# A spectral convolution and two gated MLPs: the second convolution in 20 units, in written order, and tiles 4 and 5 as a fourth pair

## The chip, the cores and the metric

The kernel runs on one core of one Trainium2 chip. A core has a matrix engine (TensorE, PE below), which multiplies out of SBUF into the eight banks of PSUM; three engines for everything else, VectorE (DVE), ScalarE (ACT) and GpSimd (POOL); and SyncE (SP), which here issues most of the transfers from and to memory. Each engine works off its own list of instructions in order and waits for the others by semaphores. The metric is the device time of one execution in microseconds, lower is better.

## The reference

The input x is 2 x 3008 x 256. A circular convolution over the 3008 positions is followed by two gated MLPs on the 6016 rows:

```python
X = np.fft.rfft(x, axis=1)
y = np.fft.irfft(X * (filt_r + 1j * filt_i)[None], n=3008, axis=1)   # 2 x 3008 x 256
t = y.reshape(6016, 256)
t = (1.0 / (1.0 + np.exp(-(t @ w_gate))) * (t @ w_val)) @ w_out      # d_ff 1536
h = t @ w_in                                                         # d_ff 2048
out = (h * (1.0 / (1.0 + np.exp(-1.702 * h)))) @ w_out2
```

The weights come as 64-bit floats and are decoded on the chip. To keep the precision, an operand is held as two parts, a high part (rounded by ACT) and a low part (the rest, by a subtraction on DVE or POOL), and a product is three matmuls, high by high, high by low and low by high (`mm3`, L123 to L126).

## The kernel before

**Tiles.** The 6016 rows are twelve tiles, six for each of the two sequences; two of each six have 480 columns instead of 512 (tiles 4, 5, 10 and 11). A tile of the first MLP needs, for each of twelve f-blocks of 128, 18 matmuls: the gate product `pg` and the value product `pv` (two row halves, three matmuls each: 12), and the back product with `w_out` (6). Around them a sigmoid on ACT, the gate product on DVE (`sg`, L591), the high part `g` on ACT (L120) and its low part `g` on POOL (L121). The back product of a unit is issued on PE two units later (`push`, `depth`).

**Pairs.** Tiles 6 to 11 are handled two at a time: the 2 x 2 blocks of weights and of the pair's columns are multiplied by seven block products instead of eight. One f-block of a pair then costs 21 matmuls and 12 for the back products, instead of 2 x 18. It needs sums of the pair's columns (`Forms`), each in two parts, and sums of the weight blocks (`combine_w1`, for each f-block one sum of 512 columns, `whole`, four of 128 and their parts). `Forms` and weight sums are done as small pieces ("chores") between the products of the sets before.

**The stage that the change touches.** The first sequence is convolved at the head, so its tiles 0 to 5 are ready. While PE multiplies tiles 2 to 5, the second sequence is convolved: the class `Conv` with steps `a1` (transform of a group's x, by `four`, whose results DVE transposes and splits into the parts `ap`), `c1` (three matmuls; ACT copies the halves swapped into `v`, DVE multiplies by the filter's real part, L536, POOL `v` by its imaginary part, L537, DVE adds both, and `yp` are the two parts of the sum), `d1` (three matmuls, and a transposition `z`) and `e1` (`four` again; two transpositions `tt` and the stores). `c1` and `d1` come 16 times, `a1` and `e1` eight times. The filter's rows are spread by copies on ACT and given their sign on POOL (`sign_f`, L394 to L398).

There are 44 units in the stage: tiles 2 and 3 with ten f-blocks each, tiles 4 and 5 with twelve. One step of the convolution is spread over two units, `a1` and `d1` in one and `c1` and `e1` in the other, so that the 16 steps take 40 units. `c1` writes bank 7, `d1` bank 6, `a1` banks 3 and 6, `e1` banks 7 and 3; `pg` and `pv` take banks 0 to 2 in turn, and the back products 4 and 5. In this stage the framework's scheduler decides the order on each engine; behind it (and in the head) the order is the written one. The weight sums of the first two f-blocks (`sum_ahead`) come in units 35 to 38, the forms of the first pair (tiles 6 and 7) in the units after the convolution. The unit loop is:

## Time and profile before

| | |
|---|---|
| median of 3 runs | 1146.67 us (1145.49 to 1146.74) |
| the profiled execution's own time | 1145.9 us |
| its span, first to last instruction | 1144.1 us |
| PE busy | 1134.6 us, 99% |
| DVE busy | 675.5 us, 59% |
| ACT busy | 646.1 us, 56% |
| POOL busy | 406.5 us, 36% |

The profile is of one execution. The span is what the rows of the trace fill; some 1.8 us lie around it. A matmul's row in the trace is longer than its share of the time, because the next one is started before it ends: what it costs is read from start to start. A DVE or ACT row overlaps its successor by some 0.1 us for the same reason. An engine's busy row can hold waiting: an instruction that has begun and is held up counts as busy.

### The profile page before, as it was taken

The page shows a single profiled execution, that of the slowest core. Times are in us where ns is not written, and L with a number is a line of the kernel's source. Part 1 is how long each engine was busy: PE and PEld are TensorE (multiplying, and loading weights), DVE is VectorE, ACT ScalarE, POOL GpSimd, SP SyncE. Part 2 cuts the span into 40 slices and gives each one's busy share as a digit, 9 for nine tenths or more (in the row PEclk, how much of TensorE's full clock was granted, in tenths as well). Part 3 has the DMA queues.
Part 4 walks back from the last instruction along what each step waited for, and adds up shares of the span by engine and source line. Part 5 has one row for each costly group of instructions (what it writes and reads, how often), then busy time and mean ns, then how long its engine had stood idle before and what let it go on. Part 6 is the DMA issues. An engine that isn't in the chain of part 4 may idle for free.

```text
span 1144.1 us, 14519 instructions
## 1 busy us (share of the span) xinstructions
PE 1134.6 (99%) x5108; PEld 912.7 (80%) x5108; DVE 675.5 (59%) x1154; ACT 646.1 (56%) x1226; POOL 406.5 (36%) x338
## 2 busy tenths in 40 slices
PE   9999999999999999999999999999999999999998
PEld 4378887777788788888888888888888888888887
DVE  6989985564655788787788789533324233233221
ACT  4655555544543555655565676656556555565554
POOL 4810004444433211211211122244555544455443
PEclk9999999999999999999999999999999999999999
DMA  9755236252512200136057251010100200200101
GB/s 205 199 183 176 92 126 144 72 100 81 97 38 74 72 3 1 38 106 125 1 188 236 83 189 33 9 66 1 49 26 1 72 1 1 74 1 1 38 1 35
DMA packets 80169, 86.75 MB, mean 76 GB/s; under 512 B 38304, under 2 KB 51104, under 8 KB 80096
## 3 DMA queue, kind: packets, MB, share of 16 engines
q1 hardware_dynamic: 78128, 82.88, 25.7%
q10 hardware_dynamic: 1968, 2.94, 0.8%
q8 instruction: 40, 0.66, 0.2%
q14 instruction: 33, 0.27, 0.1%
HBM read 54.08 MB, written 30.93 MB: 74 GB/s over the span
## 4 chain that ended last, share of the span: by engine, by line
PE 93%; DVE 2%; issue 2%; ACT 1%; DMA 1%; POOL 1%; SPq 0%; DVEq 0%; POOLq 0%; ACTq 0%
PE ps L124 30%; PE ps L125 30%; PE ps L126 30%; PE ps L324 2%; PE ps L480 1%; DMA f<-in_fd_dram 0%; PE ps L436 0%; DMA tabs<-in_tab_dram 0%; DVE sg L591 0%; DMA x<-in_xd_dram 0%; DVE yp L121 0%; DVE z L489 0%; PE ps L482 0%; DVE yp L1073 0%; ACT sg L582 0%
## 5 line engine op out<-in xcount | busy, mean ns | idle before, releaser
L121 POOL TENSOR_TENSOR g<-sg,g 128x512 fp32r<-128x512 f32 (+1 forms) x80 | 102.7, 1283 | 323.4 <-ACT g L120 319.7
L1545 POOL TENSOR_TENSOR g<-sg,g 128x512 fp32r<-128x512 f32 (+1 forms) x117 | 149.8, 1295 | 172.3 <-ACT sg L1542 169.6
L124 PE MATMUL ps<-yp,wg 128*128 128x512 f32 (+1 forms) x442 | 172.1, 390 | 0.0
L126 PE MATMUL ps<-yp,wg 128*128 128x512 f32 (+1 forms) x442 | 170.7, 386 | 0.0
L125 PE MATMUL ps<-yp,wg 128*128 128x512 f32 (+1 forms) x442 | 170.5, 386 | 0.0
L1621 DVE TENSOR_TENSOR ps<-ps,tabs 128x512 f32<-128x512 f32 (+1 forms) x48 | 33.0, 688 | 215.2 <-PE ps L126 215.2
L1541 ACT ACTIVATE g<-ps 128x512 fp32r<-128x512 f32 (+1 forms) x128 | 76.1, 595 | 85.1 <-DVE ps L1623 58.3
L125 PE MATMUL ps<-g,wo 128*128 128x512 f32 (+1 forms) x288 | 111.1, 386 | 0.5 <-POOL g L121 0.5
L124 PE MATMUL ps<-g,wo 128*128 128x512 f32 (+1 forms) x288 | 111.6, 389 | 0.0
L126 PE MATMUL ps<-g,wo 128*128 128x512 f32 (+1 forms) x288 | 110.8, 386 | 0.0
L1545 POOL TENSOR_TENSOR wo<-sg,wo 128x512 fp32r<-128x512 f32 (+1 forms) x59 | 75.7, 1292 | 84.1 <-ACT sg L1542 83.3
L1542 ACT ACTIVATE sg<-ps 128x512 f32<-128x512 f32 (+1 forms) x176 | 104.7, 595 | 1.0 <-POOL g L1545 0.7
L124 PEld LDWEIGHTS ps<-yp,wg 128*128 128x128 f32 x442 | 82.9, 188 | 23.2 <-DVE sg L591 5.7
L126 PEld LDWEIGHTS ps<-yp,wg 128*128 128x128 f32 x442 | 82.9, 188 | 16.3
L125 PEld LDWEIGHTS ps<-yp,wg 128*128 128x128 f32 x442 | 82.9, 188 | 14.8 <-issue 0.2
L120 ACT ACTIVATE g<-sg 128x512 fp32r<-128x512 f32 (+1 forms) x80 | 49.6, 620 | 70.3 <-DVE sg L591 50.0
L125 PE MATMUL ps<-g,wg 128*128 128x512 f32 (+1 forms) x192 | 74.1, 386 | 0.3 <-POOL g L1545 0.3
L126 PE MATMUL ps<-g,wg 128*128 128x512 f32 (+1 forms) x192 | 74.0, 385 | 0.0
L124 PE MATMUL ps<-g,wg 128*128 128x512 f32 (+1 forms) x192 | 74.0, 385 | 0.0
L124 PEld LDWEIGHTS ps<-g,wo 128*128 128x128 f32 x288 | 54.0, 188 | 16.7 <-issue 6.5
L582 ACT ACTIVATE sg<-ps 128x512 f32<-128x512 f32 (+1 forms) x72 | 42.2, 587 | 40.2 <-PE ps L126 32.6
L125 PEld LDWEIGHTS ps<-g,wo 128*128 128x128 f32 x288 | 54.0, 188 | 11.4 <-POOL g L121 1.3
(303 smaller groups left out, 2609.3 us busy)
## 6 DMA issues: line engine op xcount, KB each, us to landing
yraw<-xscr SPq DMA_DIRECT2D x16, 512.0 KB, 4.1
yscr<-tt SPq DMA_DIRECT2D x56, 128.0 KB, 2.1
raw<-in_w_out_dram SPq DMA_DIRECT2D x14, 512.0 KB, 3.9
x<-in_xd_dram SPq DMA_DIRECT2D x32, 192.0 KB, 4.5
wscr<-wl SPq DMA_DIRECT2D x24, 256.0 KB, 2.1
wg<-wscr SPq DMA_DIRECT2D x24, 256.0 KB, 2.9
xscr<-yraw SPq DMA_DIRECT2D x10, 512.0 KB, 3.1
f<-in_fd_dram SPq DMA_DIRECT2D x23, 192.0 KB, 3.9
```

The costliest lines, as they stand in the source:

```text
L120: nc.scalar.activation(out=dst_hi, in_=src, func=AF.Copy)
L121: lo_eng.tensor_sub(dst_lo, src, dst_hi.bitcast(F32))
L124: nc.tensor.matmul(out=o, lhsT=w[0], rhs=x[0], start=first, stop=False, **kw)
L125: nc.tensor.matmul(out=o, lhsT=w[0], rhs=x[1], start=False, stop=False, **kw)
L126: nc.tensor.matmul(out=o, lhsT=w[1], rhs=x[0], start=False, stop=last, **kw)
L324: nc.tensor.matmul(out=o[c], lhsT=w[64 * r:64 * r + n], rhs=x(r, k), start=True, stop=True, tile_position=(64 * r, 64 * k),)
L480: nc.tensor.matmul(out=o, lhsT=tbl("t3"), rhs=y, start=True, stop=not two)
L582: nc.scalar.activation(out=sg[:, :n], in_=sig_src[:, :n], func=AF.Sigmoid, scale=scale)
L1541: nc.scalar.activation(out=self.gp[0], in_=self.bank, func=AF.Gelu_apprx_sigmoid)
L1542: nc.scalar.activation(out=self.sg, in_=self.bank, func=AF.Gelu_apprx_sigmoid)
L1545: (nc.vector if self.own else nc.gpsimd).tensor_sub(self.gp[1], self.sg, self.gp[0].bitcast(F32))
L1621: nc.vector.tensor_add(y, x, s5[:, :n])
```

## The change

The second convolution is done in 20 units instead of 40, those of tiles 2 and 3, and the order on PE, ACT, DVE and POOL is written by hand there too. Every unit now holds a `c1` (of the step before) and a `d1` (of the step before that), and `a1` in even units or `e1` in odd ones. `c1` and `d1` share bank 7; `a1` and `e1` share banks 3 and 6. `c1` is cut in two: the sum and the parts follow later in the unit (`c1_sum`, `low`), and the low parts of `a1` are taken from a list. The steps of the first four units are placed one by one. The order of the accumulators of tiles 0 and 1 is swapped, and the additions that empty tile 1's are put into unit 2.

Tiles 4 and 5 leave the unit loop and become the first of now four pairs (`FIRST`). Its forms are built in place in units 10 to 19, and the weight sums of the first two f-blocks move to units 4 to 11; for all later f-blocks `whole` goes from DVE to POOL, and their weight sums are done during the new pair instead of during tiles 6 and 7. The filter's second group is loaded before the stage. The core of the diff:

```diff
-            for u in (1, 0):
+            for u in range(2):
                 a = self.fw.tile([P, 16, 32], F32, tag="a", name="a", bufs=2)
                 nc.vector.transpose(a.rearrange("p c k -> p (c k)"), banks[u])
-                ap = self.pair([P, 16, K1], "ap", 2)
-                split(*ap, a[:, :, :K1], nc.vector)
+                ap = self.pair([P, 16, K1], "ap", 4)
+                self.highs.append(lambda ap=ap, a=a: nc.scalar.activation(out=ap[0], in_=a[:, :, :K1], func=AF.Copy))
                 self.st[2 * g + u] = ap
+                self.lows.append(lambda ap=ap, a=a: nc.vector.tensor_sub(ap[1], a[:, :, :K1], ap[0].bitcast(F32)))
...
-            v = self.fw.tile([P, 16, K1], F32, tag="v", name="v", bufs=1)
+            v = self.fw.tile([P, 16, K1], F32, tag="v", name="v", bufs=2)
             nc.scalar.activation(out=v[:64], in_=pxv[64:], func=AF.Copy, scale=-1.0)
             nc.scalar.copy(v[64:], pxv[:64])
-            y = self.fw.tile([P, 16, K1], F32, tag="y", name="y", bufs=1)
+            y = self.fw.tile([P, 16, K1], F32, tag="y", name="y", bufs=2)
             nc.vector.tensor_mul(y, pxv, fr)
             nc.gpsimd.tensor_mul(v, v, fi)
+            self.st[j] = y, v
+
+        def c1_sum(self, j):
+            y, v = self.st[j]
             nc.vector.tensor_add(y, y, v)
-            yp = self.pair([P, 16, K1], "yp")
-            split(*yp, y, nc.vector)
+            yp = self.pair([P, 16, K1], "yp", 2)
+            nc.scalar.activation(out=yp[0], in_=y, func=AF.Copy)
             self.st[j] = yp
 
...
+            self.lows.append(low)
+
+        def low(self):
+            if self.lows:
+                self.lows.pop(0)()
+
+        def high(self):
+            if self.highs:
+                self.highs.pop(0)()
+
-        def d1(self, j):
+        def d1(self, j, bank=7):
             g, u = divmod(j, 2)
-            pz = ps[6]
+            pz = ps[bank]
...
-            banks = ps[7], ps[3]
+            banks = ps[3], ps[6]
...
-        acc = accs[t % 2 if t < 2 or (t < 4 and f < FK) else 0]
+        acc = accs[t % 2 if f < FK else 1 - t % 2 if t < 2 else 0]
...
+                if t == 1:
+                    ended.append(end)
...
+    conv.load_f(1)
...
-            nc.vector.tensor_add(
+            eng.tensor_add(
...
-            at_unit(35 + (5 * f + u) // 3, lambda f=f, u=u: sum_ahead(f, u))
-    for t in range(2, 6):
-        for f in range(FK if t < 4 else 0, FC1):
...
-                for lag, half, step in ((1, 0, conv.a1), (2, 0, conv.d1), (1, 1, conv.c1), (3, 1, conv.e1)):
...
-            s12(t, f, cur, lambda: run(1), lambda: run(2))
...
+            at_unit(4 + (5 * f + u) * 4 // 5, lambda f=f, u=u: sum_ahead(f, u))
...
+    ends = {2 * g + 5: g for g in range(6)} | {16: 6, 18: 7}
+    pre = []
+    for t in range(2, 4):
+        for f in range(FK, FC1):
+            pg, pv = front_bank(), front_bank()
+            m = tiles[t][3]
+            c = unit - 1 if 0 <= unit - 1 < NCH else None
+            a = 0 if unit == 1 else unit // 2 if unit and unit % 2 == 0 and unit // 2 < 8 else None
+            if c is not None and unit > 2:
+                conv.c1(c)
+            if unit == 3:
+                conv.c1_sum(1)
+                conv.low()
+            if a is not None and unit > 1:
+                conv.a1(a)
+            if unit in ends:
+                conv.e1(ends[unit])
+            for k in range(2):
+                s12_mm(t, f, cur, pg, 0, k)
+            if unit != 2:
+                conv.high()
+            sg = work.tile([P, 512], F32, tag="sg", name="sg")[:, :m]
+            nc.scalar.activation(out=sg, in_=pg[:, :m], func=AF.Sigmoid)
+            if unit != 2:
+                conv.high()
+            if unit == 2:
+                conv.c1(0)
+                conv.high()
+                conv.high()
+                ended[0](0)
+                conv.low()
+                ended[0](1)
+            elif unit == 3:
+                conv.d1(0, 3)
+                conv.c1_sum(2)
+                conv.low()
+            elif unit > 3:
+                if c is not None:
+                    conv.c1_sum(c)
+                    if a is not None:
+                        conv.low()
+                if 0 <= unit - 2 < NCH:
+                    conv.d1(unit - 2)
+            if 2 < unit < NCH:
+                conv.spread_f(unit)
+                conv.sign_f(unit, nc.gpsimd)
+            for k in range(2):
+                s12_mm(t, f, cur, pv, 1, k)
+            if unit == 2:
+                conv.c1(1)
+                conv.spread_f(2)
+                conv.sign_f(2, nc.gpsimd)
+                conv.c1_sum(0)
+            elif unit == 3:
+                conv.d1(1)
+            nc.vector.tensor_mul(sg, pv[:, :m], sg)
+            gp = [work.tile([P, 512], F32R, tag=f"g{i}", name=f"g{i}", bufs=4)[:, :m] for i in range(2)]
+            split(*gp, sg, nc.gpsimd)
+            if unit > 3:
+                conv.low()
+                conv.low()
+            if unit == 0:
+                conv.spread_f(0)
+                conv.sign_f(0, nc.gpsimd)
+            if unit == 1:
+                conv.a1(0)
+                conv.high()
+                conv.high()
+                conv.low()
+                conv.low()
+                conv.spread_f(1)
+                conv.sign_f(1, nc.gpsimd)
+            elif unit == 2:
+                conv.low()
+                conv.low()
+            if t == 2 and f in (7, 9):
+                split_y_hi(3, raw, nxt, f // 9)
+                split_y_lo(3, raw, nxt, f // 9, vec)
             for step in later.pop(unit, ()):
                 step()
+            chore(pre)
+            if unit > 16:
+                for _ in range(unit - 16):
+                    chore(pre)
+            push(s12_back(t, f, gp))
...
+                if f == 11:
+                    k01 = new_parts()
+                    n = tiles[4][3]
+                    fs = Forms([[h[:, 0] for h in k01], [h[:, 1] for h in k01]] + [None] * 5, n, y45 * 2, True)
+                    fs.dst[2], fs.dst[3] = ([packed(w, n) for w in k] for k in (ks, xk))
+                    pre += [lambda: fs.hi(0), lambda: (fs.lo(0), fs.hi(1)), lambda: fs.lo(1, nc.gpsimd)]
...
+                if f == 6:
+                    pre += [lambda: (w1(), fs.hi(4)), lambda: (fs.lo(4, nc.gpsimd), w2(), fs.hi(5), fs.hi(2))]
+                    pre += [lambda: (fs.lo(5), w4(), fs.lo(2, nc.gpsimd)), lambda: (w3(), fs.hi(3)), lambda: fs.lo(3)]
...
-    sets = {3: set3, 4: setA, 5: set5}
-    AHEAD = {3: (2,), 4: (2,), 5: ()}
+    sets = {2: set3, 3: setA, 4: set5, 5: setA}
...
-    RATE = {3: (1, 2, 2), 4: (1, 2, 1), 5: (1, 2, 1)}
+    FIRST = 2
+    RATE = {2: (1, 2, 2), 3: (1, 2, 1), 4: (1, 2, 1), 5: (1, 2, 1)}
...
-    ready = set(range(PRE + 1))
+    ready = set(range(PRE))
...
-    for p in range(3, nt // 2):
+    for p in range(FIRST, nt // 2):
```

What stands in a row on DVE shows at the sixth step. Before, from the gate product of one unit over the next two: each step's product, sum and low part stand between gate products of their own. (`sg` is the gate product, `y` the product with the filter and the sum, `yp` and `ap` low parts, `tt` and `z` transpositions; the number behind `ps` is the bank.)

```order
L591 TENSOR_TENSOR sg_1928<-ps0_71,sg_1928 128x512
L536 TENSOR_TENSOR y_1951<-ps7_78,f0_1771 128x384
L538 TENSOR_TENSOR y_1951<-y_1951,v_1948 128x384
L121 TENSOR_TENSOR yp1_1956<-y_1951,yp0_1955 128x384
L591 TENSOR_TENSOR sg_1982<-ps2_73,sg_1982 128x512
L403 STREAM_TRANSPOSE tt_1975<-ps7_78 128x512
L403 STREAM_TRANSPOSE tt_1975<-ps3_74 128x512
L549 STREAM_TRANSPOSE z_2012<-ps6_77 128x512
L591 TENSOR_TENSOR sg_2020<-ps1_72,sg_2020 128x512
L536 TENSOR_TENSOR y_2039<-ps7_78,f0_1771 128x384
```

After, on the same engine, from unit 4's gate product to unit 5's `z`:

```order
L1247 TENSOR_TENSOR sg_1916<-ps2_73,sg_1916 128x512
L530 TENSOR_TENSOR ap1_1908<-a_1905,ap0_1907 128x384
L554 TENSOR_TENSOR yp1_1921<-y_1894,yp0_1920 128x384
L1057 TENSOR_TENSOR yp0_1945<-wg0_83,wg1_84 128x512
L1064 TENSOR_TENSOR yp0_1945<-yp0_1945 128x128
L1065 TENSOR_TENSOR yp0_1945<-yp0_1945 128x128
L542 TENSOR_TENSOR y_1968<-ps7_78,f0_1825 128x384
L408 STREAM_TRANSPOSE tt_1975<-ps3_74 128x512
L408 STREAM_TRANSPOSE tt_1975<-ps6_77 128x512
L548 TENSOR_TENSOR y_1968<-y_1968,v_1965 128x384
L572 STREAM_TRANSPOSE z_1927<-ps7_78 128x512
```

Two low parts and the first three instructions of the weight sums (L1057 is `whole`, L1064 and L1065 the 128-column sums) now stand between the gate product and the next product with the filter, L542, which reads bank 7.

On POOL, in the same part of the stage, before (`g` is the low part for the back product, `v` the product with the filter, `f` the sign):

```order
L121 TENSOR_TENSOR g1_1931<-sg_1928,g0_1930 128x512
L537 TENSOR_TENSOR v_1948<-v_1948,f1_1772 128x384
L121 TENSOR_TENSOR g1_1985<-sg_1982,g0_1984 128x512
L121 TENSOR_TENSOR g1_2023<-sg_2020,g0_2022 128x512
L537 TENSOR_TENSOR v_2036<-v_2036,f1_1772 128x384
L121 TENSOR_TENSOR g1_2062<-sg_2059,g0_2061 128x512
L398 TENSOR_TENSOR f1_2123<-f1_2123,tabs_88 128x384
```

And after:

```order
L543 TENSOR_TENSOR v_2031<-v_2031,f1_1826 128x384
L403 TENSOR_TENSOR f1_1957<-f1_1957,tabs_88 128x384
L121 TENSOR_TENSOR g1_2080<-sg_2056,g0_2079 128x512
L543 TENSOR_TENSOR v_2102<-v_2102,f1_1957 128x384
L403 TENSOR_TENSOR f1_1957<-f1_1957,tabs_88 128x384
L121 TENSOR_TENSOR g1_2146<-sg_2125,g0_2145 128x512
L543 TENSOR_TENSOR v_2168<-v_2168,f1_1957 128x384
L403 TENSOR_TENSOR f1_2096<-f1_2096,tabs_88 128x384
L121 TENSOR_TENSOR g1_2217<-sg_2193,g0_2216 128x512
```

Each unit's `g` now has a `v` and a sign between it and the next one; before, two units shared one of each.

On ACT at the start of the stage, before (`sg` is a unit's sigmoid, `g` its high part, the copies spread the filter's first group, which has just been loaded):

```order
L582 ACTIVATE sg_1680<-ps2_73 128x512
L120 ACTIVATE g0_1682<-sg_1680 128x512
L582 ACTIVATE sg_1708<-ps1_72 128x512
L397 COPY f0_1658<-f0_1658 64x384
L120 ACTIVATE g0_1710<-sg_1708 128x512
L397 COPY f0_1658<-f0_1658 64x384
L397 COPY f1_1659<-f1_1659 64x384 x2
```

And after:

```order
L1214 ACTIVATE sg_1681<-ps2_73 128x512
L120 ACTIVATE g0_1690<-sg_1681 128x512
L398 COPY f0_1662<-f0_1662 64x384
L398 COPY f1_1663<-f1_1663 64x384
L1214 ACTIVATE sg_1712<-ps1_72 128x512
L120 ACTIVATE g0_1721<-sg_1712 128x512
L528 ACTIVATE ap0_1731<-a_1729 128x384
```

The first two copies have moved ahead of the second unit's sigmoid.

## Rows read from the trace of the kernel before

**Rows 1.** The page's first lines: busy us, share of the span, instructions.

```profile
span 1144.1 us, 14519 instructions
...
PE 1134.6 (99%) x5108; PEld 912.7 (80%) x5108; DVE 675.5 (59%) x1154; ACT 646.1 (56%) x1226; POOL 406.5 (36%) x338
```

**Rows 2.** Busy time in two stretches: length; PE, PEld, DVE, ACT, POOL; clock, DMA share, GB/s.

```profile
25.00:50.00 25.00, 23.46 (x106) 8.55 (x105) 23.82 (x37) 17.46 (x33) 23.37 (x23) 1.00 0.89 234
...
175.00:200.00 25.00, 23.94 (x105) 17.69 (x103) 12.77 (x21) 14.06 (x27) 12.57 (x11) 1.00 0.54 130
```

**Rows 3.** The timeline of PE, three stretches: start us, us, engine, line, operation.

```profile
184.58 0.39 PE L126 MATMUL ps<-g,wo 128*128 128x512 f32 x1
...
185.94 0.39 PE L126 MATMUL ps<-yp,wg 128*128 128x512 f32 x1
...
186.69 0.40 PE L124 MATMUL ps<-yp,wg 128*128 128x512 f32 x1
...
200.31 1.09 PE L324 MATMUL ps<-x,tabs 48*64 48x512 f32 x8
...
201.66 0.39 PE L125 MATMUL ps<-yp,wg 128*128 128x512 f32 x1
...
369.97 0.37 PE L124 MATMUL ps<-yp,wg 128*128 128x480 f32 x1
...
371.27 0.37 PE L124 MATMUL ps<-yp,wg 128*128 128x480 f32 x1
```

**Rows 4.** The timeline of DVE and POOL in one step of the convolution.

```profile
218.45 0.56 DVE L536 TENSOR_TENSOR y<-ps,f 128x384 f32<-128x384 f32 x1 [2.19 <-ACT v L534]
218.56 1.02 POOL L537 TENSOR_TENSOR v<-v,f 128x384 f32<-128x384 f32 x1 [0.26 <-ACT v L534]
...
220.75 0.56 DVE L121 TENSOR_TENSOR yp<-y,yp 128x384 fp32r<-128x384 f32 x1 [0.59 <-ACT yp L120]
...
221.23 0.68 DVE L591 TENSOR_TENSOR sg<-ps,sg 128x512 f32<-128x512 f32 x1
...
222.55 1.31 DVE L521 STREAM_TRANSPOSE a<-ps 128x512 f32<-128x512 f32 x2 [0.64 <-PE ps L324]
222.65 1.30 POOL L121 TENSOR_TENSOR g<-sg,g 128x512 fp32r<-128x512 f32 x1 [3.08 <-ACT g L120]
```

**Rows 5.** The timeline where DVE and POOL meet, three stretches, with PE.

```profile
30.32 1.33 DVE L778 SCALAR_TENSOR_TENSOR c<-raw,c 128x512 uint32<-128x512 uint32 x1
...
31.06 1.44 POOL L468 TENSOR_TENSOR v<-xs,f 128x384 f32<-128x384 f32 x1
...
190.47 1.64 POOL L121 TENSOR_TENSOR g<-sg,g 128x512 fp32r<-128x512 f32 x1 [1.29 <-ACT g L120]
...
190.89 1.63 DVE L121 TENSOR_TENSOR yp<-y,yp 128x384 fp32r<-128x384 f32 x1
...
191.13 0.39 PE L124 MATMUL ps<-yp,wg 128*128 128x512 f32 x1
...
192.58 0.45 PE L125 MATMUL ps<-yp,tab 128*128 128x384 f32 x1 [1.06 <-DVE yp L121]
...
369.51 0.68 DVE L1028 TENSOR_TENSOR wex<-wg,wg 128x512 f32<-128x512 f32 x1
...
370.23 0.29 DVE L1035 TENSOR_TENSOR wc<-wex 128x128 f32<-128x128 f32 x1
370.31 1.29 POOL L121 TENSOR_TENSOR g<-sg,g 128x480 fp32r<-128x480 f32 x1 [2.67 <-ACT g L120]
...
370.55 1.20 DVE L1036 TENSOR_TENSOR wc<-wc,wex 128x128 f32<-128x128 f32 x1
```

**Rows 6.** The timeline of ACT and PE at the start of the stage.

```profile
175.76 0.60 ACT L582 ACTIVATE sg<-ps 128x512 f32<-128x512 f32 x1 [1.29 <-PE ps L126]
...
178.30 0.51 ACT L397 COPY f<-f 64x384 f32<-64x384 f32 x1 [1.95 <-DMA f<-in_fd_dram]
...
178.37 1.07 PE L324 MATMUL ps<-x,tabs 48*64 48x512 f32 x4
```

More of the change, by code (lines that the diff above doesn't have):

```diff
@@ L660, with load_part @@
     part = {}
+    ended = []
+    def load_part(t):
+        part[t] = new_raw()
+        nc.sync.dma_start(out=part[t], in_=xscr[t].rearrange("(c p) n -> p c n", p=P))
     def s12_back(t, f, gp):
         n = tiles[t][3]
[L664 removed]
+        acc = accs[t % 2 if f < FK else 1 - t % 2 if t < 2 else 0]
         first, last = f == 0, f == FC1 - 1
@@ L669, in back @@
         def back():
-            if f == FC1 - 2 and t < 4:
-                part[t] = new_raw()
-                nc.sync.dma_start(out=part[t], in_=xscr[t].rearrange("(c p) n -> p c n", p=P))
+            if f == FC1 - 2 and t != 2:
+                load_part(t)
             for c in range(2):
@@ L681, in back, with end @@
             elif last:
-                if t < 4:
-                    x2 = part[t]
-                    for c in range(2):
-                        nc.vector.tensor_add(x2[:, c, :n], x2[:, c, :n], acc[c][:, :n])
-                else:
-                    x2 = conv.fw.tile([P, 2, 512], F32, tag="x2", name="x2", bufs=1) if t == 4 else st2.tile([P, 2, 512], F32, tag="raw", name="x2", bufs=2)
-                    nc.scalar.copy(x2[:, 0, :n], acc[0][:, :n])
-                if t >= 4:
-                    nc.vector.tensor_copy(x2[:, 1, :n], acc[1][:, :n])
-                if n < 512:
-                    nc.gpsimd.memset(x2[:, :, n:], 0.0)
-                nc.sync.dma_start(out=xscr[t].rearrange("(c p) n -> p c n", p=P), in_=x2)
+                x2 = part[t]
+                def end(c):
+                    nc.vector.tensor_add(x2[:, c, :n], x2[:, c, :n], acc[c][:, :n])
+                    if c:
+                        nc.sync.dma_start(out=xscr[t].rearrange("(c p) n -> p c n", p=P), in_=x2)
+                if t == 1:
+                    ended.append(end)
+                else:
+                    end(0)
+                    end(1)
         return back
@@ L998 @@
     sx0 = [w33.tile([P, PRE * 3, P], F32R, name=f"sx0{i}") for i in range(2)]
+    xk, ks = ([w33.tile([P, 512], F32R, name=f"{k}{i}") for i in range(2)] for k in ("xk", "ks"))
     pools = ExitStack()
@@ new lines, with combos @@
+            at_unit(4 + (5 * f + u) * 4 // 5, lambda f=f, u=u: sum_ahead(f, u))
+    ctx.enter_context(
+        tc.manual_schedule(
+            engines={
+                mybir.EngineType.PE, mybir.EngineType.Activation, mybir.EngineType.DVE, mybir.EngineType.Pool,
+            }
+        )
+    )
+    def combos(f):
+        v, r = (st2.tile([P, 1, 4, P], F32, tag=k, name="w" + k) for k in ("ex", "c"))
+        return combine_w1(f, 1, v, r, nc.gpsimd)
+    ends = {2 * g + 5: g for g in range(6)} | {16: 6, 18: 7}
@@ L1184 @@
             for step in later.pop(unit, ()):
                 step()
-            if pools is not None and k == NCH + 3:
+            chore(pre)
[3 more added lines that the diff above has]
+            push(s12_back(t, f, gp))
+            g, odd = divmod(unit, 2)
+            if odd == 0 and 1 < g + 1 < 8:
+                conv.load_f(g + 1)
+            if odd == 1 and g + 2 < 8:
+                conv.load_x(g + 2)
+            if unit == 18:
@@ L1218 @@
-                one, two, three, four = fs.inplace()
-                def combos(f):
-                    v, r = (st2.tile([P, 1, 4, P], F32, tag=k, name="w" + k) for k in ("ex", "c"))
-                    return combine_w1(f, 1, v, r)
-                w2 = lazy(lambda: combos(PRE))
-                pre = [w2, lambda: (fs.hi(0), fs.hi(1)), lambda: (fs.lo(0), one(), fs.hi(4)), lambda: fs.lo(1)]
-                pre += [lambda: (fs.lo(4), two(), fs.hi(5)), lambda: (fs.hi(2), fs.lo(5)), lambda: (fs.lo(2), three())]
@@ L1227 @@
-                pre += [lambda: fs.hi(6), four, lambda: (fs.lo(6), fs.hi(3)), lambda: fs.lo(3)]
-            elif pools is None:
-                for _ in range(4):
-                    chore(pre)
+                fs.dst[6] = [packed(w, n) for w in kr]
+                pre += [lambda: fs.hi(6), lambda: fs.lo(6)]
             unit += 1
-            if t < 5:
+            if t == 2:
                 if f == 3:
-                    raw = load_y(t + 1)
-                if f == 7:
+                    raw = load_y(3)
+                if f == 6:
@@ L1415, in prod @@
                 mm3(o, lhs[k], rhs[k], first, True, skip_group_check=True)
-            first_set = p == 3 and f == 0
+            first_set = p == FIRST and f == 0
             if first_set:
-                chores += [lazy(lambda q=q: weights(q)) for q in range(PRE + 1, FC1)]
-            if p == 3:
+                chores += [lazy(lambda q=q: weights(q)) for q in range(PRE, FC1)]
+            if p == FIRST:
                 while f not in ready:
```

71 lines of the change are left out of this document (24 added, 47 removed).

## The prediction

> **What bounds the kernel now.** I read the page's busy times first. TensorE (PE) is busy 1134.6 of 1144.1 us, DVE 59%, POOL 36% [rows 1]: PE sets the time, so the change is priced in two things, matmuls that PE no longer issues and microseconds in which PE will wait. Next I read PE's own timeline for the price of a matmul. Six of 512 columns take 185.94 - 184.58 = 1.36 us, 0.227 each; three of 384 columns take 0.75 less one of those, 0.52; six of 480 columns take 1.30, 0.217 each [rows 3]. The eight records of one `four` transform, with the switch of data type around them, take 201.66 - 200.31 = 1.35 less a 512-column matmul, 1.12, and some 0.1 before them: 1.2 [rows 3]. In the stage of the second convolution PE hardly waits; the one wait of size is 1.06 us, and from 191.13 to 192.58, with the restarts, it costs 1.4 us over a matmul's own time [rows 5].
>
> Then I read that wait, since it shows what else is scarce. POOL began `g` at 190.47 and was at it for 1.64 us instead of 1.30 [rows 4, 5]; DVE's low part `yp`, 0.56 us when alone, began at 190.89 and took 1.63, and PE stood until it was done [rows 4, 5]. The same at 370: a 128-column subtraction of DVE's, 0.29 when alone, took 1.20 while POOL held a low part [rows 5]. So DVE instructions that read two tiles of SBUF and POOL's instructions exclude each other. They also take turns: at 30.32 DVE waited out one POOL instruction and then POOL's next one, begun at 31.06, took 1.44 instead of the 1.02 of a like product [rows 4]; at 370.31 POOL got in between two back-to-back instructions of DVE [rows 5]. A DVE instruction whose data come from PSUM is not held: two transposes took 1.31 with POOL's `g` beside them [rows 4].
>
> **The change, part by part.**
>
> *Fewer matmuls.* Tiles 4 and 5 needed 18 matmuls each per f-block; as a pair they need 21 + 12. 12 x 3 = 36 fewer of 480 columns: 36 x 0.217 = **-7.8 us**, on the path. The convolution's own matmuls stay as many. The wait at 191 goes with the old order: **-1.4**.
>
> *The convolution at double density.* A unit on PE is now 18 x 0.227 + 6 x 0.173 + 1.2 = 6.3 us. In it DVE has three transposes, the gate product, the filter product L542, one sum, two low parts in even units and one in odd ones: by the rows 4 to 5 us, which fits. POOL has a sign (as long as `v`, 1.02: same shape), `v` and `g`: 1.0 + 1.0 + 1.3 = 3.3 where it had about half. The throughput fits; the order is the question. Both products of a step now go to bank 7: `c1` writes it at the unit's start, L542 on DVE must read it, then `d1` writes it. PE reaches `d1` at 0.5 + 1.2 + 1.4 = 3.1 us of the unit. What DVE has queued between the gate product of one unit and L542 of the next therefore has to be done 9.4 us after the first unit's start (6.3 + 3.1), or PE stands; `d1`, and behind it the value matmuls and the back product, wait with it.
>
> Take an even unit, from its start. `c1` ends at 0.5, `four` at 1.7, two transposes (1.3) at 3.1, the sum at 3.6; ACT's `yp` high and its two 0.51 us copies of `f` [rows 6] end at 5.7, and POOL's sign starts. The value matmuls end at 5.2, the gate product at 5.9, POOL's `g` could start at 6.7 (1.4 after the gate product's start: 221.23 to 222.65 [rows 4]). From 5.7 on everything queues for the same thing in turn: sign 1.0, low part `ap` 0.5, `g` 1.3, low part `yp` 0.5 (220.75 to 221.23 [rows 4]), and then, in units 4 and 8, the 512-column sum of two weight tiles, 0.6 [rows 5], two 128-column sums, 0.5, and POOL's next `v`, 1.0, between them. 5.7 + 5.4 = 11.1, and L542 takes until 11.7: PE waits **2.3**. Units 6 and 10 have two 128-column subtractions there (0.4 for 1.1): 1.6. Odd units start the queue with `yp` at 5.9; in 5 and 7 the low part of tile 3 (0.6) waits for ACT and comes behind `g`, then `v`, then the small sums: 5.9 + 0.5 + 1.0 + 1.3 + 0.6 + 1.0 + 0.5 = 10.8, with L542 11.4: 2.0 and 1.9. Unit 9 has two small ones: 9.1, with L542 9.7: 0.3. Unit 11 has those, a low part of the fourth pair (0.6), `v` and the two additions that empty tile 2's accumulators (1.3): 12.0, 12.6: 3.2. Sum 2 x 2.3 + 2 x 1.6 + 2.0 + 1.9 + 0.3 + 3.2 = **+15.2**. No trace shows this order, so both ends: if DVE kept its turn against POOL's last two instructions, an even unit would read 5.7 + 1.0 + 0.5 + 0.5 + 0.6 + 0.5 + 0.6 = 9.4 and cost nothing: 0. If each wait also shifts the next unit's sign and `v` into the way, up to 0.7 more at each of the eight: 20.8. I take 15.2, since every meeting in the rows was in turns.
>
> *The plain units.* Without extra work an even unit's L542 ends at 9.6: 0.2 each; in unit 16 an in-place subtraction on DVE stands behind a low part that POOL makes after its `g`. Together **+1.0** (0 to 2.4).
>
> *The start.* ACT's copies of `f` waited for their load until 178.30; the second unit's sigmoid went ahead at 175.76 [rows 6]. Now the sigmoid stands behind two of the copies: 178.30 + 1.0 = 179.3, 3.6 us later. Behind it on ACT are `g` and the high parts, on DVE the gate product (to 180.0) and both transposes (to 181.9); PE comes to the second `four`, which overwrites their banks, six matmuls and one `four` after the first. The first was at 178.37 [rows 6] and is now six matmuls earlier, so the second is due at 179.6: PE waits 2.2. In units 2 and 3 sixteen DVE instructions with the same turns follow; I count 1.0 for them, up to 4.5, or nothing: **+3.2** (2.2 to 6.7).
>
> *The rest.* PRE chores, the loads and the fourth pair's first set hide as the third pair's did: weight sums for two f-blocks are ready before the stage ends, and the others run under 33 x 0.217 = 7.2 us of matmuls per block, with POOL taking the 512-column sum from DVE. The old hand-over to the first pair had some 2 us of short waits; I keep them. The added pair boundary counts as nothing; without the cover of its low parts made ahead it would cost one high and low part, some 1.2.
>
> The sum: -7.8 - 1.4 + 15.2 + 1.0 + 3.2 = +10.2 on the profiled execution's 1145.9 (span 1144.1 and 1.8 around it), 1156.1. The median of the runs is 0.8 above it: **1157**.
>
> PE would now stand some 19 us of 145, in pieces of 2. The clock was 1.00 in 25:50, where PE was idle for 1.5 of 25, and in 175:200 with its wait [rows 2]. The Trainium skill, "TensorE: Matmul & The Clock Gate" (A second HAM failure mode: psum-queue depth-cycling), says that short idling of PE between groups of matmuls can make its clock swing between the two levels; the trace shows no such swing. By the rows the sum has nothing for it; by that rule it would have the price of the third rival.
>
> **The rivals.**
> *The waits are hidden: faster.* The mechanism is DVE's queue: if at the crossings DVE's small instructions get their turns before POOL's `g` and `v`, L542 is done by 9.4 and nothing reaches PE. It decides at one point, whether the weight sums run before or after `v`. Against it stand the turns at 30 and 370; for it, that throughput fits and `d1` has 2 us of air in plain odd units. -7.8 - 1.4 + 3.2 = -6.0: 1140.7; with no wait at the start either, 1137.5.
> *Half of them:* 7.6 for 15.2: +2.6, 1149.
> *Clock.* If the granted clock fell to 1.2 GHz for a third of the stage, some 42 us of matmuls would take twice as long: 1197.
> *Waits pile up* to the upper ends, 20.8 and 6.7: +19.3, 1166.
> *The change does not do what it says:* the order has 36 PE rows fewer and the stage in 20 units, so this is all but out.
>
> **How the numbers follow.** Forecast 0.41, pile-up 0.10, half 0.12, hidden 0.33, clock 0.03, nothing 0.01. Within 0.2% (2.3 us, about what a measurement of this kernel can tell from no change) lies a part of "half" and "nothing": 0.06. Faster: hidden and the lower edge of half, 0.36. Slower: 0.58. Both signs have weight, so the range goes from the hidden case without waits to the pile-up, 1137 to 1166; that leaves out the clock and the tails. The likeliest case alone is 1150 to 1163.
>
> **What would show it.** In PE's waits of the changed kernel: `ps L124` on DVE's `y` L542, some 2 us each at `d1` of units 5 to 12; DVE low parts of over 1 us beside POOL; PE's busy share down to some 85% between 180 and 320 us; a 2 us wait of the second `four` at the start. I am wrong if L542 of units 5 to 12 starts within 1.5 us of `c1`'s end, or if POOL lets two DVE instructions pass in a row.

## The result, and the profile after

The changed kernel takes 1160.32 us (median of 4 runs, 1159.56 to 1162.36); the kernel before took 1146.53 beside it. The ratio is 1.0125, with a 95% interval of 1.0107 to 1.0142: 13.8 us slower. The profiled execution is the longest of the four, 1162.4 us with a span of 1160.5, which is 16.4 above the span of before [rows 1].

The page's first lines, span and busy times, as in [rows 1]:

```profile
span 1160.5 us, 14600 instructions
...
PE 1135.2 (98%) x5072; PEld 907.5 (78%) x5072; DVE 724.0 (62%) x1193; ACT 657.7 (57%) x1253; POOL 415.6 (36%) x341
```

PE has 36 matmuls fewer, as the diff says, and is still busy 98%. So the page alone hides what happened; the list of what PE waited for, by the line that it waited with and the instruction that released it (us in total, times, longest), names it:

```profile
PE ps L124 <- DVE y L542: 10.7, 8, 2.2
PE ps L324 <- DMA x<-in_xd_dram: 1.8, 1, 1.8
PE ps L124 <- DVE ps L1562: 1.0, 2, 0.8
PE ps L124 <- DVE z L572: 0.9, 1, 0.9
PE ps L124 <- DVE ps L1578: 0.7, 1, 0.7
PE ps L125 <- DVE yp L554: 0.7, 2, 0.4
```

`L542` is DVE's product with the filter, and `ps L124` behind it is `d1`: the wait that the prediction put first. The busy times of four stretches (length; PE, PEld, DVE, ACT, POOL; clock, DMA share, GB/s) show where, and show a second thing that [rows 2] did not have, a granted clock under 1.00:

```profile
175.00:200.00 25.00, 22.32 (x86) 14.53 (x84) 14.16 (x24) 12.45 (x26) 10.74 (x9) 0.86 0.62 155
200.00:225.00 25.00, 21.32 (x109) 14.26 (x107) 22.30 (x34) 15.28 (x34) 11.99 (x10) 1.00 0.26 69
225.00:250.00 25.00, 20.75 (x105) 13.78 (x98) 23.96 (x34) 13.41 (x28) 12.60 (x11) 1.00 0.65 127
250.00:275.00 25.00, 21.77 (x99) 15.17 (x99) 22.49 (x35) 13.74 (x29) 11.57 (x11) 0.93 0.49 105
```

To see what each thing costs I took PE's rows from start to start, subtracted the pitch of each shape ([rows 3]: 0.227, 0.217 and 0.173 us; 1.02 for a `four`, 177.79 to 178.81), and put each excess down to the wait that the row names, or to the clock where the pitch doubles. A wait's excess holds its restart too, the slower start of the matmuls around it: 1.78 us for the 1.61 us of idle time at 212.60. From unit 0's first matmul to some 10 us past the first one of tiles 6 and 7:

| excess over the matmuls' own time, us | before | after |
|---|---|---|
| waits for L542 | - | 12.0 |
| slow clock, two stretches | - | 5.4 |
| second `four`, wait for x | - | 1.9 |
| units 2 to 4: waits for `yp` and `z` | - | 2.2 |
| the wait at 191 [rows 5] | 1.2 | - |
| pair boundaries | 1.3 | 2.7 |
| other restarts | 0.3 | 1.0 |
| pieces under 0.15 | 5.5 | 7.4 |
| sum | 8.3 | 32.6 |

24.3 more excess and 7.8 less work make 16.5; from unit 0's first matmul to the first of tiles 6 and 7 it grew from 215.45 to 232.18, by 16.7. Of the rest of the 16.4, unit 0 starts 0.8 later (the first `four` of the kernels below, whose heads are alike, scatters between 176.49 and 178.51, so that need not be the change's), and from tile 6 on the kernel is 1.1 shorter.

**The crossing itself.** DVE and POOL between unit 4's gate product and unit 5's L542, and unit 5's gate product (the timeline; start us, us, engine, line, operation):

```profile
207.49 1.15 POOL L403 TENSOR_TENSOR f<-f,tabs 128x384 f32<-128x384 f32 x1 [2.77 <-ACT f L398]
207.68 1.38 DVE L554 TENSOR_TENSOR yp<-y,yp 128x384 fp32r<-128x384 f32 x1
...
208.60 1.60 POOL L121 TENSOR_TENSOR g<-sg,g 128x512 fp32r<-128x512 f32 x1
208.98 1.77 DVE L1057 TENSOR_TENSOR yp<-wg,wg 128x512 f32<-128x512 f32 x1
...
210.16 1.45 POOL L543 TENSOR_TENSOR v<-v,f 128x384 f32<-128x384 f32 x1
...
210.78 0.97 DVE L1064 TENSOR_TENSOR yp<-yp 128x128 f32<-128x128 f32 x1
...
211.79 0.29 DVE L1065 TENSOR_TENSOR yp<-yp 128x128 f32<-128x128 f32 x1
212.00 0.55 DVE L542 TENSOR_TENSOR y<-ps,f 128x384 f32<-128x384 f32 x1
...
214.89 0.69 DVE L1247 TENSOR_TENSOR sg<-ps,sg 128x512 f32<-128x512 f32 x1
```

This is the queue of the order listing. Alone these DVE instructions take 0.56, 0.68 and 0.29 us [rows 4, 5]; here 1.38, 1.77 and 0.97: each waits out one of POOL's three instructions, and POOL's wait in their turn (1.60 and 1.45 for 1.30 and 1.02). The last small one takes 0.29, because POOL has run out. PE, meanwhile (its timeline, in three places):

```profile
180.07 0.40 PE L126 MATMUL ps<-g,wo 128*128 128x512 f32 x1
182.24 2.46 PE L324 MATMUL ps<-x,tabs 48*64 48x512 f32 x8 [1.77 <-DMA x<-in_xd_dram]
184.63 0.80 PE L124 MATMUL ps<-yp,wg 128*128 128x512 f32 x1
...
210.60 0.40 PE L126 MATMUL ps<-yp,wg 128*128 128x512 f32 x1
212.60 0.45 PE L124 MATMUL ps<-yp,tab 128*128 128x384 f32 x1 [1.61 <-DVE y L542]
...
265.15 0.40 PE L126 MATMUL ps<-yp,wg 128*128 128x512 f32 x1
267.72 0.49 PE L124 MATMUL ps<-yp,tab 128*128 128x384 f32 x1 [2.18 <-DVE y L542]
...
268.65 0.63 PE L124 MATMUL ps<-yp,wg 128*128 128x512 f32 x1
269.08 0.63 PE L125 MATMUL ps<-yp,wg 128*128 128x512 f32 x1
```

At 212.60 `d1` starts 1.77 us late. At 267.72, behind the longest of these waits, the pitch is 0.43 instead of 0.227 (268.65 to 269.08): the clock's lower level, 1.2 GHz, for 3.8 us. The same at 182.24 behind the wait for x, where a `four` takes 2.39 us and the slow stretch lasts until 189.5.

### The profile page after: what moved, and what is told of

Same layout as the page of the kernel before. It is cut to its first block, busy times and chain, and to the rows that moved or that the text cites. A ratio compares the mean times of both kernels' runs of the same rounds, so it can differ in the third digit from the quotient of the medians.

```text
span 1160.5 us, 14600 instructions
## 1 busy us (share of the span) xinstructions
PE 1135.2 (98%) x5072; PEld 907.5 (78%) x5072; DVE 724.0 (62%) x1193; ACT 657.7 (57%) x1253; POOL 415.6 (36%) x341
## 4 chain that ended last, share of the span: by engine, by line
PE 87%; DVE 6%; DMA 3%; issue 2%; ACT 1%; SPq 0%; POOL 0%; DVEq 0%; POOLq 0%; ACTq 0%
PE ps L124 28%; PE ps L125 28%; PE ps L126 28%; DMA x<-in_xd_dram 1%; PE ps L324 1%; DMA f<-in_fd_dram 1%; DVE yp L554 1%; PE ps L485 1%; DVE yp L1102 0%; DVE sx L1074 0%; DVE y L542 0%; DMA tabs<-in_tab_dram 0%; PE ps L441 0%; DVE tt L408 0%; DVE yp L1057 0%
## 5 line engine op out<-in xcount | busy, mean ns | idle before, releaser
L121 POOL TENSOR_TENSOR g<-sg,g 128x512 fp32r<-128x512 f32 (+1 forms) x68 | 89.8, 1320 | 372.7 <-ACT g L120 366.8
L1635 POOL TENSOR_TENSOR g<-sg,g 128x512 fp32r<-128x512 f32 (+1 forms) x117 | 149.9, 1294 | 172.2 <-ACT sg L1632 169.6
L124 PE MATMUL ps<-yp,wg 128*128 128x512 f32 (+1 forms) x382 | 151.1, 396 | 0.0
L125 PE MATMUL ps<-yp,wg 128*128 128x512 f32 (+1 forms) x382 | 149.2, 391 | 0.0
L126 PE MATMUL ps<-yp,wg 128*128 128x512 f32 (+1 forms) x382 | 149.1, 390 | 0.0
L124 PE MATMUL ps<-g,wo 128*128 128x512 f32 (+1 forms) x288 | 111.1, 387 | 0.1
L1632 ACT ACTIVATE sg<-ps 128x512 f32<-128x512 f32 (+1 forms) x176 | 104.8, 595 | 1.1 <-POOL g L1635 0.8
L124 PEld LDWEIGHTS ps<-yp,wg 128*128 128x128 f32 x382 | 72.5, 190 | 27.3 <-issue 13.8
L126 PEld LDWEIGHTS ps<-yp,wg 128*128 128x128 f32 x382 | 72.4, 190 | 14.6
L125 PEld LDWEIGHTS ps<-yp,wg 128*128 128x128 f32 x382 | 72.4, 190 | 13.4 <-issue 0.2
L124 PE MATMUL ps<-g,wg 128*128 128x512 f32 (+1 forms) x192 | 74.0, 385 | 0.0
L1569 ACT ACTIVATE sg<-ps 128x480 f32<-128x480 f32 (+1 forms) x48 | 28.1, 586 | 71.6 <-DVE ps L1567 71.6
L120 ACT ACTIVATE g<-sg 128x512 fp32r<-128x512 f32 (+1 forms) x68 | 42.4, 623 | 40.2 <-DVE sg L1591 29.3
L124 PEld LDWEIGHTS ps<-g,wo 128*128 128x128 f32 x288 | 54.2, 188 | 11.8 <-issue 0.8
L1602 DVE TENSOR_TENSOR g<-ps,g 128x480 fp32r<-128x480 f32 (+1 forms) x48 | 32.4, 675 | 49.1 <-ACT g L1599 48.9
```

The lines of the kernel that those rows point to most:

```text
L120: nc.scalar.activation(out=dst_hi, in_=src, func=AF.Copy)
L121: lo_eng.tensor_sub(dst_lo, src, dst_hi.bitcast(F32))
L124: nc.tensor.matmul(out=o, lhsT=w[0], rhs=x[0], start=first, stop=False, **kw)
L125: nc.tensor.matmul(out=o, lhsT=w[0], rhs=x[1], start=False, stop=False, **kw)
L126: nc.tensor.matmul(out=o, lhsT=w[1], rhs=x[0], start=False, stop=last, **kw)
L1569: nc.scalar.activation(out=sgz, in_=z, func=AF.Sigmoid)
```

## Experiments

**Do turns with POOL make the waits?** My theory is that POOL's instructions are inserted into DVE's queue one by one. The rival is that DVE's own queue is simply too long. The edit takes only POOL's work away: it leaves out the filter's sign from unit 3 on.

```diff
                 conv.spread_f(unit)
-                conv.sign_f(unit, nc.gpsimd)
```

> Leaves out the sign of the filter's imaginary part from unit 3 on (13 POOL instructions of about 1.0 us; nothing of DVE's or PE's own list changes). My theory (DVE instructions with two SBUF inputs and POOL's instructions take turns, so POOL's time is added to DVE's queue ahead of L542): the eight waits for L542, 12.0 us with their restarts, fall to 3 to 7 us, the DVE low parts and sums in these units get shorter by the turns that are gone, and the time falls to about 1152 to 1156. Rival (DVE's own work ahead of L542 is too much, whatever POOL does, or ACT's high parts set the time): the waits stay at 10 to 12 us and the time at 1159 to 1161.

Measured, in one run: 1147.84 us, and the waits for L542 come to 4.1 with their restarts (3.3 without). DVE and POOL in the same place as above:

```profile
203.46 0.55 DVE L554 TENSOR_TENSOR yp<-y,yp 128x384 fp32r<-128x384 f32 x1
...
203.93 0.69 DVE L1057 TENSOR_TENSOR yp<-wg,wg 128x512 f32<-128x512 f32 x1
203.93 1.82 POOL L121 TENSOR_TENSOR g<-sg,g 128x512 fp32r<-128x512 f32 x1 [3.44 <-ACT g L120]
...
204.65 1.25 DVE L1064 TENSOR_TENSOR yp<-yp 128x128 f32<-128x128 f32 x1
...
205.71 1.06 POOL L543 TENSOR_TENSOR v<-v,f 128x384 f32<-128x384 f32 x1
...
205.93 0.99 DVE L1065 TENSOR_TENSOR yp<-yp 128x128 f32<-128x128 f32 x1
...
206.84 0.55 DVE L542 TENSOR_TENSOR y<-ps,f 128x384 f32<-128x384 f32 x1
```

DVE's list is the same; `yp` now takes 0.55, and `whole`, which starts together with POOL's `g`, 0.69 (`g` takes 1.82); the two small sums then wait for `g` and `v` as before. So POOL's presence makes the lengths, as the theory said. The time fell further than I had expected, since no stretch of slow clock is left in this profile (PE's clock is 1.00 from 175 to 325): of the 14.5 us by which it lies below the profiled execution of the changed kernel, 7.9 are the waits for L542 and 5.4 the slow stretches.

**Order or throughput?** By the rows a unit with a weight sum needs about 3.3 us of POOL and 3 us of DVE instructions with two SBUF inputs, almost the 6.4 us that it lasts. If that binds, another order doesn't help. The edit issues the same pieces behind the next unit's L542:

```diff
             if c is not None and unit > 2:
                 conv.c1(c)
+            for step in later.pop(unit - 1, ()):
+                step()
...
-            for step in later.pop(unit, ()):
-                step()
             chore(pre)
```

> Only the place of the weight sums in units 4 to 11 changes: each unit's piece is issued behind the next unit's L542 instead of ahead of it; work and counts stay. My theory (order: what counts is what stands on DVE ahead of L542): the waits of PE for L542, 12.0 us with their restarts over eight units, fall to 4 to 7 (the low part of tile 3 in units 5 and 7 and the emptying of tile 2's accumulators in unit 11 stay where they are), and little comes back elsewhere; time 1150 to 1155. Rival (throughput: POOL's 3.3 us and some 3 us of DVE instructions with two SBUF inputs fill a unit of 6.4 us, so the delay only moves on, to the parts of y, to z or to the next unit's L542): the waits sum to 10 us or more again under other names; time 1158 to 1161.

Measured, in one run: 1153.22 us. PE's waits in the stage:

```profile
PE ps L124 <- DVE z L572: 3.4, 6, 0.9
PE ps L124 <- DVE y L542: 2.8, 5, 0.8
```

The waits for L542 fell from 10.7 to 2.8, those for `z` rose from 0.9 to 3.4: of some 8 us about a third came back under another name. The theory's time held, and its "little comes back" was too good: order is the larger cause, and a full unit is a real one beside it. The time itself proves less than the waits do: this execution has no stretch of slow clock either, and that is worth 5.4 of the 9.1 us by which it lies below the profiled execution of the changed kernel.

**The start of the stage.** The trace of the changed kernel names the load of x for the second `four`, where I had forecast ACT's copies. The rows there, on SP, ACT and DVE:

```profile
171.90 2.40 SPq L351 DMA_DIRECT2D f<-in_fd_dram  x4
...
174.35 1.51 SPq L344 DMA_DIRECT2D x<-in_xd_dram  x2
...
179.32 0.51 ACT L398 COPY f<-f 64x384 f32<-64x384 f32 x1 [0.40 <-DMA f<-in_fd_dram]
...
179.86 0.60 ACT L1214 ACTIVATE sg<-ps 128x512 f32<-128x512 f32 x1
...
180.49 0.69 DVE L1247 TENSOR_TENSOR sg<-ps,sg 128x512 f32<-128x512 f32 x1 [4.62 <-ACT sg L1214]
181.10 1.30 DVE L526 STREAM_TRANSPOSE a<-ps 128x512 f32<-128x512 f32 x2
```

Both chains end within 0.3 us of each other. SP issues the second group's x behind all four loads of the filter (at 174.35; before, at 172.27), and it landed 7.76 us later, at 182.11. The copies of the filter hold the sigmoid until 179.86, and DVE's transposes behind it end at 182.40. One edit swaps the loads, one moves the copies and the sign of unit 0 behind unit 1's high parts, and one kernel has both:

```diff
     conv.load_x(0)
     conv.load_f(0)
-    conv.load_f(1)
     conv.load_x(1)
+    conv.load_f(1)
...
-            if unit == 0:
-                conv.spread_f(0)
-                conv.sign_f(0, nc.gpsimd)
...
-                conv.spread_f(1)
-                conv.sign_f(1, nc.gpsimd)
+                for j in range(2):
+                    conv.spread_f(j)
+                    conv.sign_f(j, nc.gpsimd)
```

> Only the order of two loads on SP changes: the x of the second group is loaded ahead of the filter's second group. In the changed kernel PE stood 1.94 us before the second `four` (182.24); the trace names the load of x, which landed at 182.11, but the transposes on DVE, held back by ACT's copies of the filter, ended only 0.3 us later than that start. My theory (the copies on ACT ahead of the sigmoid hold the chain): the wait stays at 1.5 us or more and is put down to DVE `a` L526; the granted clock still falls behind it; time 1159 to 1161. Rival (the load alone is the cause): the wait goes, the clock stays at 2.4 GHz, time 1155 to 1156.

> Only the place of four instructions changes: the copies and the sign of the filter's first half stand behind the second unit's sigmoid and the high parts instead of ahead of them. My theory (two causes that end within 0.3 us of each other): DVE's transposes are done by about 180, but PE still waits for the load of x until 182.1, so the wait stays at about 1.8 us; time 1159 to 1161. Rival (the copies alone, and the load is early enough): the wait goes, time 1155 to 1158.

> Both edits together. My theory: the wait before the second `four` shrinks from 1.94 us to under 0.5, which gives 1.5 to 1.9 us; if the clock's fall behind it (182.2 to 189.5, some 3.0 us) hangs on that wait, it goes too, and the time is about 1155.5; if the fall hangs on something else, it stays and the time is about 1158.5. Rival (the stage's start is bound by the filter's load or by DVE): units 2 and 3 wait longer instead, time 1160.

Measured: 1162.26 with the loads alone and 1159.52 with the copies alone (one run each), 1159.44 (1158.0 to 1161.18, 4 runs; ratio to before 1.0125, interval 1.0109 to 1.0142) with both. The second `four` on PE's timeline, first with the loads swapped:

```profile
181.25 2.01 PE L324 MATMUL ps<-x,tabs 48*64 48x512 f32 x8 [1.85 <-DVE a L526]
```

With the copies moved:

```profile
180.72 1.59 PE L324 MATMUL ps<-x,tabs 48*64 48x512 f32 x8 [1.04 <-DMA x<-in_xd_dram]
```

With both:

```profile
180.89 1.54 PE L324 MATMUL ps<-x,tabs 48*64 48x512 f32 x8
```

PE waits 1.85 for the transposes, 1.04 for x, and with both edits not at all. So there were two causes, each hidden behind the other. For the copies alone I had expected a wait for x of 1.8; with the start left as it was, the two kernels above waited 1.31 and 0.97 for it, so the size of this wait varies whether the copies are moved or not. The median hardly shows the gain, and the 1155.5 that I had expected with both was missed. The profiled run of the kernel with both has no slow stretch and took 1158.0 us, but its waits for L542 are 12.2 us, 1.5 more than in the changed kernel: unit 2 has a new one of 0.5, and unit 16's is 1.37 instead of 0.42. The longest is 2.19 us, as in the changed kernel. Its four runs scatter by 3 us, and the clock is at most a part of that: the mean clocks are 1.000, 0.998, 0.998 and 0.997, and the two runs with 0.998 took 1161.18 and 1158.17.

**Moving the work out of the way.** If all this holds, the weight sums belong where POOL is idle, and other pieces behind L542. The first kernel has both edits at the start and puts the first f-block's sums into units 0 and 2, the second one's into odd units; the second also moves tile 3's high parts, the emptying of tile 2 and the start of the last forms:

```diff
-            at_unit(4 + (5 * f + u) * 4 // 5, lambda f=f, u=u: sum_ahead(f, u))
+    for u, k in enumerate((9, 9, 11, 13, 15)):
+        at_unit(k, lambda u=u: sum_ahead(1, u))
...
             push(s12_back(t, f, gp))
+            if unit == 0:
+                for u in range(2):
+                    sum_ahead(0, u)
...
                 conv.a1(a)
+            if unit == 2:
+                for u in range(2, 5):
+                    sum_ahead(0, u)
```

The second has besides:

```diff
-            if t == 2 and f in (7, 9):
-                split_y_hi(3, raw, nxt, f // 9)
+            if t == 2 and f in (6, 8):
+                split_y_hi(3, raw, nxt, f // 8)
+            if t == 2 and f in (7, 9):
                 split_y_lo(3, raw, nxt, f // 9, vec)
...
                 conv.c1(c)
+            if unit == 12:
+                ended[1](0)
+                ended[1](1)
...
-                if f == 6:
+                if f == 8:
                     pre += [lambda: (w1(), fs.hi(4)), lambda: (fs.lo(4, nc.gpsimd), w2(), fs.hi(5), fs.hi(2))]
```

> Both edits at the stage's start as in the run before with both, and the weight sums leave units 4 to 8 and 10: those of the first f-block go to units 0 and 2, where DVE stood idle for some 2 us each (176.4 to 178.4 and 183.3 to 185.8 in that run), those of the second to the odd units 9 to 15, which have no transform of x and so two low parts fewer. My theory: L542's waits in units 5, 7, 9 and 11 go, those in 6, 8 and 12 (the low part of tile 3, the accumulators) stay at 1.3, 1.3 and 1.7 to 2.3, with 0.6 to 1.5 in unit 17: 5 to 7 us in place of 13; against 1159.4 with both start edits that is 1151 to 1153, and 2 to 3 us less if the clock falls less often behind shorter waits. Rival (the small sums cost as much wherever they stand, a turn of POOL each): the waits move to units 10 to 16 and sum to 10 us or more; time 1156 or more.

> The run before and three more moves: the high part of tile 3 is issued a unit earlier than its low part, the emptying of tile 2's accumulators stands behind unit 12's L542, and the second half of the fourth pair's forms is begun two units later, when no filter product is left. My theory: L542's waits sum to 1 to 4 us; what is left of idle PE is the start's 3 to 4 us and the two pair boundaries; time 1146 to 1149, the same as before the change. Rival: the forms that now crowd units 17 to 19 make the first products of the fourth pair wait by 2 us or more, and the time stays over 1150.

Measured: 1150.74 (1148.79 to 1151.77; ratio 1.0037, interval 1.0024 to 1.0050) and 1147.67 (1146.92 to 1150.27; ratio 1.0018, interval 1.0008 to 1.0027). PE's waits for L542 in the stage, in the first kernel:

```profile
PE ps L124 <- DVE y L542: 5.3, 4, 2.0
```

And in the second:

```profile
PE ps L124 <- DVE y L542: 1.2, 2, 1.0
```

The first has the sum that I expected in other places: units 6 and 8 no longer wait at all, so their waits came from the sums and the turns behind them, and not from tile 3's low part alone; unit 10 waits 1.2 behind `whole`, which I had left in unit 9. The second kernel's profiled execution is the slowest of its ten and has a stretch of slow clock at the start, behind a wait of 1.05 for x. (What the expectations here and below put in units 17 and 9 are the waits at the `d1` of units 16 and 10.)

Three more moves, and then one at the pair boundaries:

```diff
     conv.load_x(0)
-    conv.load_f(0)
     conv.load_x(1)
+    conv.load_f(0)
...
-    for u, k in enumerate((9, 9, 11, 13, 15)):
+    for u, k in ((1, 9), (2, 11), (3, 13), (4, 15)):
...
             if unit == 2:
                 for u in range(2, 5):
                     sum_ahead(0, u)
+                sum_ahead(1, 0)
...
                 conv.c1_sum(2)
-                conv.low()
...
                 conv.d1(1)
+                conv.low()
...
-                nf.lo(4)
+                nf.lo(4, nc.gpsimd)
...
-                nf.lo(1, nc.gpsimd)
+                nf.lo(1)
```

> The run with all moves, and three more: the two loads of x stand ahead of both loads of the filter; the 512-column sum of the second f-block goes from unit 9 to unit 2; in unit 3 the low part of the third y stands behind the transposition z of the second one, on which unit 4's first matmul waited 0.9 us. My theory: the wait of 1.19 us (with its restart) in unit 9 falls to under 0.3, that of 1.08 at unit 4's start to under 0.3, the second `four` waits under 0.3 for its x, and with no wait over 1 us left in the stage the clock falls in fewer runs: 1144 to 1146.5. Rival (the turns move on to the sum of the third y and to unit 2's L542): the same waits under other names, 1147 to 1148.

> The run before, and in the last block of each pair one low part of the next pair's forms goes from DVE to POOL and another from POOL to DVE, so that one instruction of 0.6 us less stands on DVE ahead of the sum that PE waits for. My theory: the second wait at the boundary behind tiles 4 and 5 (0.86 us) falls by 0.5, and as much or less at the other two boundaries: 0.5 to 1.3 us faster than the run before. Rival: the low part on POOL takes a turn ahead of DVE's next one, so the waits stay: no difference.

Measured: 1144.71 (1144.36 to 1145.93, 11 runs; ratio to before 0.9994, interval 0.9985 to 1.0004) and 1143.99 (1143.38 to 1145.5, 11 runs; 0.9987, 0.9977 to 0.9996). The last kernel is the only one whose interval lies below the kernel before, by 0.13% in the middle. PE's waits in it:

```profile
PE ps L124 <- DVE y L542: 1.8, 2, 1.6
PE ps L125 <- DVE yp L554: 0.7, 2, 0.4
PE ps L124 <- DVE z L572: 0.5, 1, 0.5
```

The waits in unit 10 and at unit 4's start are gone, and one has taken their place, as the rival said: unit 2's L542, 1.6 us, behind the sums that I put there (ACT's last high part of them, held up by a small sum of 1.10 us beside POOL's sign, stands ahead of `v`). The boundary move did not do what I expected. Its rows on POOL and DVE:

```profile
382.33 1.43 POOL L1102 TENSOR_TENSOR yp<-xs,yp 128x512 fp32r<-128x512 f32 x1 [3.30 <-ACT yp L1097]
...
383.10 1.21 DVE L1102 TENSOR_TENSOR yp<-xs,yp 128x512 fp32r<-128x512 f32 x1
...
384.23 0.65 DVE L1586 TENSOR_TENSOR ps<-ps,tabs 128x480 f32<-128x480 f32 x1
...
384.94 0.48 PE L124 MATMUL ps<-xk,wg 128*128 128x480 f32 x1 [0.64 <-DVE ps L1586]
```

POOL's new low part and DVE's next one begin 0.8 us apart and take 1.43 and 1.21: a turn again. PE's wait behind them fell by 0.07 only. What makes the last kernel's median 0.7 lower than the one before it, its trace doesn't show (the spans are 1142.6 and 1142.8); the two intervals overlap, so there may be nothing to explain, and I leave that open.

## Why the prediction was right, and where not

The forecast was 1157, with the likeliest case from 1150 to 1163 and the whole range from 1137 to 1166, and it came out at 1160.3. The signs it named are there: waits of 1.2 to 2.3 us for L542 at seven of the eight `d1`, low parts of over 1 us beside POOL, PE 83 to 89% busy in the four stretches, and 1.77 us before the second `four`. Neither sign of being wrong is: in units 5 to 12 L542 starts at least 1.6 us behind `c1`'s end, and DVE and POOL alternate. By its steps:

**Fewer matmuls, -7.8: right.** 5072 instead of 5108. The last kernel shows the gain by itself: its excess in the stage is 14.8 where that of before is 8.3, so +6.5 - 7.8 = -1.3, and its span is 1.5 shorter. The old wait, -1.4, is gone too.

**The convolution at double density, +15.2: the mechanism right, the size a third too high.**

| L542 of unit | 5 | 6 | 7 | 8 | 9 | 10 | 11 | 12 | sum |
|---|---|---|---|---|---|---|---|---|---|
| forecast | 2.3 | 2.0 | 1.6 | 1.9 | 2.3 | 0.3 | 1.6 | 3.2 | 15.2 |
| measured | 1.77 | 1.33 | 1.35 | 1.32 | 2.08 | 0 | 1.23 | 2.34 | 11.4 |

The experiments show the cause: without POOL's signs the waits come to 4.1, with the sums behind L542 to 3.6, with the sums elsewhere and the other moves to 1.5. Two things made the forecast too high. In unit 5 the queue ended 11.4 us after unit 4's start instead of 11.7, and PE came to `d1` after 9.6 instead of 9.4. And from unit 6 on I counted each wait as if the unit before had none: unit 5's wait moved PE by 1.77, but DVE's queue only by 1.3 (its gate product began at 214.89, 7.2 after the unit's start instead of 5.9). The Trainium skill, "SBUF — State Buffer" (SBUF: two separate sides), states what the turns are: a DVE instruction with two SBUF inputs and a GpSimd instruction that reads SBUF share one pair of ports, and whoever issues first has it for the whole instruction. The trace agrees (1.38 for 0.56). Who gets the pair next when both have work queued I read from the rows alone: they alternate.

**The plain units, +1.0:** 0.6, all of it in unit 16, but by another way than I wrote: the in-place subtraction takes 1.47 us beside POOL's sign and `g`, ACT's high part of its result stands ahead of the next `v`, and L542 comes behind `v`.

**The start, +3.2: too low, and half its cause missed.** Measured were 1.9 for the second `four` and 2.2 for units 2 to 4, with 0.5 of restarts: 4.7 in all. The term that was too small is the 1.0 for units 2 and 3; the 2.2 for the second `four` was near. The chain through ACT's copies was there as forecast, but the load of x ended as late as that chain. The step that failed is the one that hid "the loads": I had not followed SP's queue, on which two loads of the filter had moved ahead of x.

**The clock, 0 in the sum: wrong by 5.4 in this execution.** I took "the trace shows no such swing" for the answer, and gave the fall only as a rival of 42 us with a chance of 0.03 (its 1197 should be 1199: 1157 and 42). It is not all or nothing: PE falls to 1.2 GHz for 3 to 7 us behind some of its waits. The rule that the prediction set beside the rows, of the Trainium skill, "TensorE: Matmul & The Clock Gate" (A second HAM failure mode: psum-queue depth-cycling), that short idling of PE can make its clock swing, went the right way: the clock fell behind the waits of 1.77 and 2.18 us, though not behind that of 1.91. The trace of before, which had one wait of 1.06 in the stage, could not show it.

**The rest, 0:** the boundary behind the new pair costs 1.9 (0.99 and 0.87) where the sum has nothing and I had named 1.2 without its cover, and the pair's own start 1.1; the old hand-over, which I kept, had 1.6. Net 1.4. (The 1.1 and the 1.6 each hold a piece of 0.3 that the table above has under other restarts.)

So the mechanism was right, but that the total came so close is partly luck, since its errors offset each other: L542 3.8 lower, the plain units 0.4, against 5.4 of clock, 1.4 at the boundaries, 1.5 at the start and about 2 in small pieces. Without the two slow stretches this execution would have been near 1157.

## What to carry to other kernels

When two uses of one buffer are put an engine's queue apart, list what stands between them on that queue, and count for each DVE instruction with two SBUF inputs one of POOL's as well, as long as POOL has any. Put work that nobody waits for where the other engine is idle, or behind the instruction that frees the buffer: the same instructions cost 12 us of waits for L542 in one order and 3.6 (with 2.5 more of waits for `z`), or 1.5, in another. Follow the queue of loads as carefully as the engines, since a load that was early enough can be 2 us late when another is put ahead of it.
